# Routed attention and a cosine router on one core: gates of early blocks written ahead of a weight load, the first wide item's sums and rows ahead of the gates' parts

## The chip, the cores and the metric

One core of a Trainium2 chip runs the whole program in one launch. The core has five engines, each with its own list of instructions in a fixed order: PE (matmuls; PEld loads its stationary operand), DVE (element work and 32x32 transposes), ACT (activations and copies), POOL (element work, and DMAs whose rows are picked by a list of numbers) and SP (it only issues DMAs). An engine waits at an instruction until what it needs has come, and everything behind that instruction on the same engine waits too. The metric is the time of one execution in microseconds, as the median of several. Three runs before took 655.72 to 656.14, median 655.92.

## The reference

```python
# attention: every query sees only the keys of its own cluster
mask = q_assign[:, :, :, None] == k_assign[:, :, None, :]      # argmax over 16 unit centroids
scores = np.where(mask, scale * np.matmul(q, k.transpose(0, 1, 3, 2)), -1000000000.0)
attn = softmax(scores); x = np.matmul(attn, v)                 # (4, 8, 768, 64) -> rows (3072, 512)
# router: one of 8 experts for each row, by cosine
logits = xn @ en.T / tau
expert_idx = np.argmax(logits, axis=1); gate_w = probs[np.arange(N), expert_idx]
for e in range(E):                                             # w1[e]: 512x1024, w2[e]: 1024x512
    h = np.maximum(x[mask] @ w1[e], 0.0)
    out[mask] = gate_w[mask, None] * (h @ w2[e])
```

`softmax` stands for the three lines that shift, exponentiate and divide. All values are float32.

## The kernel before, in words

The attention works through 4 batches of 8 heads, 768 tokens each, and writes its rows to memory as `x_rows`. While it does, the rows of batches that are done are routed. Behind the attention come the experts, as a row of items, each with one expert's two weight tables, `w1s` and `w2s` (2 MB each, two buffers of each, loaded by `weights1` and `weights2`):

- Three early items (`E0[0]` to `E0[2]`) of 128 rows each, taken from the first 12 of 24 row blocks (`SA` of `NSLOT`), which are routed before the attention ends. Their work on PE is `hidden` (line 1653, 64 matmuls) and `result` (line 1694, 8 matmuls). The output rows are scaled by `gatein`, a gate for each row, and scattered to `out` by POOL.
- Eight sized (wide) items (`sized[0]` to `sized[7]`), one for each expert, of 392 down to 248 rows. Each product is done with seven half-size products in place of eight, so sums of quarters of the weights (`w1_sums`, lines 1390 to 1393) and of the rows (`x_sums`, lines 1365 to 1368) are made on DVE first.
- One block more at the end, and a branch (`overflow`) for rows that fit nowhere. With these inputs the branch isn't entered, but each engine loads `used` and compares.

The places of all rows are worked out by `Places(1)`, called `pb`, once the last batch is routed: `ranks`, `firsts` and `dest` on DVE; `hot_blocks` (`rr25b`, half on POOL at line 1026, half on DVE at line 1027) and `hot_rows` (`ohrb`, line 1033); `tokens`, 24 matmuls at line 1044 that turn these two into token numbers; `token_rows`, which writes the lists `gidx` and `sidx` by which POOL gathers the first wide item's rows (`collect`). The gates of all rows go the same way: `gate_parts` splits each gate into three bfloat16 parts, `hot_gates` (line 1071) makes the operand `rg25b`, and `gates` multiplies it (24 matmuls, line 1080). `spread_gates` (line 1622) lays the result out for the wide items.

The gates of the first three batches take a second way, for the early items: `gate_pieces` turns them, SP writes them to memory as `gate_rows` (line 809, four DMAs of 18 rows of 128 bytes), and `fetch_gate` gathers them on POOL (line 1138).

The first wide item's rows are not read back transposed. They are gathered on the chip, put in order by DVE (`order_rows`, line 1330) and turned by PE (`turn_rows`, line 1348). The rows of the second wide item are gathered, written to memory (`lay`, line 1243) and read back (`bring`, line 1260); SP can't issue the read before the write has landed.

What sets the order is the text of the kernel: `manual_schedule` is on for all five engines, so each engine's list is the order in which the calls stand. The engines meet only through semaphores.

Of the kernel before, what the change touches and what calls it, by code (L numbers as in the profile page):

```python
# [39 lines left out]
def kernel(  # L40
# [1136 lines left out]
    def weights1(it, parts=1):  # L1177
        it.e = expert_of(it)
        for i in range(parts):
            load_part(w1s[it.slot], moe_w1, it.e, KD, i, parts)  # L1180
# [98 lines left out]
    def fetch_gate(it):  # L1279
        gate = mo[it]["gate"] = xip.tile([P, 1], F32, tag="gatein", name="gatein", bufs=4)  # L1280
        gather(gate, gate_rows[0 : SA * P], gidxs[0][:, it.j : it.j + 1], SA * P)
# [7 lines left out]
    def turn_x(it, evict=None, xT=None):  # L1289
        d = mo[it]  # L1290
        if it.kind == "sized":
            n = WIDE[it.j]
            d["xT"] = szp.tile([P, KD, SQ * max(WIDE)], F32, tag="xTs", name="xTs", bufs=1)
            for u in range(0, n, NQ):
                m = min(NQ, n - u)
                nc.vector.transpose(
                    d["xT"][:, :, SQ * u : SQ * u + SQ * m].rearrange(
                        "p c (w t) -> p w c t", t=SQ
                    ),
                    d["xs"][:, u : u + m].rearrange("p w (c i) -> p w c i", i=SQ),  # L1300
                )
            return
        d["xT"] = mop.tile([P, DM], F32, tag="xTm", name="xTm") if xT is None else xT
        if it.kind == "block" or it in E0[1:]:
            nc.vector.transpose(
                d["xT"].rearrange("p (c w t) -> p w c t", c=KD, t=SQ),
                d["xin"].rearrange("p w (c i) -> p w c i", i=SQ),
            )
            return
        bk = psX.tile([P, DM], F32, tag="x_ps", name="x_ps")  # L1310
        for c in range(KD):
            nc.tensor.transpose(
                bk[:, P * c : P * c + P], d["rows"][:, c].rearrange("p w i -> p (w i)"), ident
            )
        evict(d["xT"], bk)

    def order_rows(it):

        d = mo[it]
        spare = szp.tile([P, max(WIDE), P], F32, tag="ys", name="ordered", bufs=YB)  # L1320
        spare = spare.rearrange("p u x -> p (u x)")
        d["ordered"] = []
        for i, (x, _) in enumerate(d.pop("rows_in")):
            n = x.shape[0]
            if DM * i + DM <= spare.shape[1]:
                to = spare[0:n, DM * i : DM * i + DM]
            else:
                to = szp.tile([P, FH, HC], F32, tag="hS1", name="ordered", bufs=1)
                to = to.rearrange("p f t -> p (f t)")[0:n, 0:DM]
            nc.vector.tensor_copy(  # L1330
                to.rearrange("p (c w i) -> p c w i", c=KD, w=NQ),
                x.rearrange("p (w c i) -> p c w i", c=KD, w=NQ),
            )
            d["ordered"].append(to)
# [35 lines left out]
    def x_sums(it):  # L1370

        d, h = mo[it], CAPS[it.j] // 2
        sums = d["xS"] = [
            szp.tile([P, KH, HC], F32, tag=f"xS{i}", name=f"xS{i}", bufs=1)[:, :, 0:h]
            for i in (1, 2, 4)
        ]
        four_sums(halves(it), sums)
# [6 lines left out]
    def w1_sums(it):  # L1384

        (b11, b12), (b21, b22) = quarters(w1s[it.slot])
        t2, t3, t4 = mo[it]["t1"] = [
            szp.tile([P, KH, F // 2], F32, tag=f"t1{i}", name=f"t1{i}", bufs=1) for i in (2, 3, 4)
        ]
        nc.vector.tensor_tensor(t3, b22, b12, ALU.subtract)  # L1390
        nc.vector.tensor_tensor(b12, b12, b11, ALU.subtract)
        nc.vector.tensor_tensor(t2, b22, b12, ALU.subtract)
        nc.vector.tensor_tensor(t4, b21, t2, ALU.subtract)
# [243 lines left out]
    def hidden(it, halves=(0, 1), span=(0, 512)):  # L1637

        d = mo[it]
        for half in halves:  # L1640
            if half == 0 and span[0] == 0:
                if it.kind == "whole":
                    t = szp.tile([P, KD, SQ * max(WIDE)], F32, tag="yT", name="hT", bufs=1)
                    d["hT"] = t.rearrange("p g t -> p (g t)")[:, 0:F]
                else:
                    d["hT"] = mop.tile([P, F], F32, tag="hT", name="hT")
            f0 = 512 * half
            if span[0] == 0:
                d["h_ps"] = psH.tile([P, 512], F32, tag="h_ps", name="h_ps")
            bk = d["h_ps"]  # L1650
            for m in range(*span, P):
                for c in range(KD):
                    nc.tensor.matmul(  # L1653
                        bk[:, m : m + P],
                        lhsT=w1s[it.slot][:, c, f0 + m : f0 + m + P],
                        rhs=d["xT"][:, P * c : P * c + P],
                        start=(c == 0),
                        stop=(c == KD - 1),
                    )
            if span[1] == 512:  # L1660
                nc.scalar.activation(d["hT"][:, f0 : f0 + 512], bk, ACTF.Relu)
# [99 lines left out]
    E0 = items[0:KA]  # L1761
    later = items[KA:]
    sized, last = later[:-1], later[-1]
# [70 lines left out]
    with tc.manual_schedule(engines=by_hand):  # L1834
        begin()
        for i in range(0, len(units), 2):
            n, it = divmod(i // 2, NJ)
# [51 lines left out]
        pb = Places(1, rtb)  # L1889
# [12 lines left out]
        hidden(E0[0], (1,), (0, 256))  # L1902
        products(0, 1)
        hidden(E0[0], (1,), (256, 512))
        weights1(E0[2])
        logits(0, 1)
        choose()
        for gate in gates[1:]:
            gate()
        for it in E0:  # L1910
            fetch_gate(it)
        hidden(E0[1], (0,), (0, 256))
        pb.ranks()
        hidden(E0[1], (0,), (256, 512))
        pb.firsts()
        pb.dest(0)
        pb.dest(1)
        pb.hot_blocks()
        turn_x(E0[2])
        hidden(E0[1], (1,))  # L1920
        for j in range(NJ):
            norms(j)
# [15 lines left out]
        pb.token_rows(gidxs[1], sidxs[1])  # L1938
        collect(sized[0])
        pb.experts(True)  # L1940
        for gate in gates[1:]:
            gate()
        pb.gate_parts()
        result(E0[1])
        w1_sums(sized[0])
        pb.hot_gates(NB)
        order_rows(sized[0])
        pb.gates(slot_gates)

        def overflow():  # L1950
            n_used = nc.values_load(used[0:1, 0:1], min_val=0, max_val=KX + NO)
# [34 lines left out]
        collect(sized[1])  # L1986
        result(E0[2], (2,), 4)
        turn_rows(sized[0])
        result(E0[2], (3,), 4)
        weights2(sized[0])  # L1990
        weights1(sized[1])
        lay(sized[1])
        bring(sized[1])
        spread_gates()
        x_sums(sized[0])

        next_of = dict(zip(sized, [*sized[2:], last]))
        for k, it in enumerate(sized[:-1]):
            after = sized[k + 1]
            before = sized[k - 1] if k else None  # L2000

            def first_steps(i):
                if i == 0:
                    if before:
                        sized_rows(before)
                        put(before)
                    if k:
                        collect(next_of[it])
                        w2_copy(it, "b11")
                elif i == 1 and k:  # L2010
                    w2_sum(it, "t3")
                elif i == 2 and k:
                    w2_copy(it, "b22")

            def second_steps(i):
                if i == 0:
                    h_sums(it, 0)
                    if k:
                        w2_sum(it, "t2")
                        w2_copy(it, "b21")  # L2020
                elif i == 1 and k:
                    w2_sum(it, "t4")
                elif i == 2 and k:
                    weights2(after)
                    send(before)
                elif i < 5 and not k:
                    w2_sum(it, ("t1", "t3", "t2", "t4")[i - 1])
                    if i < 4:
                        w2_copy(it, ("b11", "b22", "b21")[i - 1])
                    else:  # L2030
                        collect(next_of[it])
                        weights2(after)

            def third_steps(i):
                if i == 0:
                    h_sums(it, 2)
                    if after is not sized[-1]:
                        w1_sums(after)
                elif i == 1:
                    turn_x(after)  # L2040
                    bring(next_of[it])
                    weights1(next_of[it])
                elif i == 3 and after is not sized[-1]:
                    x_sums(after)
                elif i == 4 and after is not sized[-1]:
                    w2_sum(after, "t1")

            sized_hidden(it, 0, first_steps)
            sized_hidden(it, 2, second_steps)
            lay(next_of[it])  # L2050
            sized_result(it, third_steps)
# [68 lines left out]
```

## Time and profile before

| | us |
|---|---|
| median of 3 runs (655.72 to 656.14) | 655.92 |
| the profiled execution | 657.54 |
| its span | 655.8 |
| PE busy | 636.8 (97%) |
| DVE busy | 497.4 (76%) |
| ACT busy | 316.9 (48%) |
| POOL busy | 164.5 (25%) |

The granted TensorE clock is 0.988 of full speed over the span. The page cuts the span into 40 slices of 16.4 us and gives each engine's busy share in tenths; a timeline gives, for each run of like instructions, its start, its length, the engine, the line, what it writes and reads, and in brackets how long the engine sat idle before it and what ended that. All times within the span are counted from its start. Lengths of matmuls reach from the first start to the modelled end of the last; a group followed without a gap ends a little after the next has begun.

### The profile page before, as it was taken

To read this page: it belongs to the slowest core of one execution; us is meant where nothing else is said; L and a number is where in the kernel's file an instruction comes from. 1 tells how busy PE (TensorE), PEld (TensorE's weight loads), DVE (VectorE), ACT (ScalarE), POOL (GpSimd) and SP (SyncE) were. 2 spreads that over 40 slices of the span, in tenths; PEclk is the share of its full clock that TensorE was granted. 3 is DMA by queue.
4 is the path that set the end of the run, shared out by engine and by line. 5 is a ranking of instruction groups with operands and counts; after the bars stand their busy time and mean duration, and the time that the engine had idled before them with its cause. 6 is when DMAs were issued, how large, how long until landed. Compare 5 with 4: busy or idle time off the path is not lost. (4 is left out here: it accounts for less than half of the span.)

```text
span 655.8 us, 16397 instructions
## 1 busy us (share of the span) xinstructions
PE 636.8 (97%) x6529; PEld 451.8 (69%) x6529; DVE 497.4 (76%) x823; ACT 316.9 (48%) x533; POOL 164.5 (25%) x360
## 2 busy tenths in 40 slices
PE   9999999999999999999995799999999999999997
PEld 4444444444444445445675369999999999999995
DVE  6988988998889999999884628677777778775210
ACT  6656655677655785667541125152525242433311
POOL 2222212312214112235704412205040404030111
PEclk9999999999999999999997899999999999999999
DMA  9855666787549678667888258877996969685753
GB/s 153 127 89 102 99 94 106 154 144 122 102 82 171 132 160 171 132 158 210 259 224 298 85 158 288 267 252 229 310 294 224 302 220 300 234 289 209 253 164 111
DMA packets 257665, 122.62 MB, mean 187 GB/s; under 512 B 208257, under 2 KB 228609, under 8 KB 257580
## 3 DMA queue, kind: packets, MB, share of 16 engines
q1 hardware_dynamic: 253116, 108.58, 65.9%
q0 software_dynamic: 4288, 12.85, 6.2%
q8 instruction: 54, 0.88, 0.6%
q14 instruction: 31, 0.25, 0.1%
q10 hardware_dynamic: 176, 0.05, 0.0%
HBM read 92.53 MB, written 23.28 MB: 177 GB/s over the span
## 5 line engine op out<-in xcount | busy, mean ns | idle before, releaser
L585 ACT ACTIVATE prob<-s_ps 128x768 f32<-128x768 f32 x192 | 154.3, 813 | 100.1 <-PE s_ps L574 97.5
L574 PE MATMUL s_ps<-qT,kT 64*64 64x384 f32 x1536 | 156.1, 483 | 0.0
L596 PE MATMUL o_ps<-prob,v 64*64 64x385 f32 x1536 | 141.3, 484 | 0.0
L615 DVE TENSOR_TENSOR acc<-acc,prob 128x768 f32<-128x768 f32 x128 | 121.4, 948 | 8.6
L596 PEld LDWEIGHTS o_ps<-prob,v 64*64 64x64 f32 x1536 | 57.6, 133 | 65.5 <-issue 58.0
L574 PEld LDWEIGHTS s_ps<-qT,kT 64*64 64x64 f32 x1536 | 55.2, 133 | 36.1 <-issue 31.9
L1149 POOL DMA_INDIRECT out_dram<-rows_out,sidx x24 | 25.4, 1059 | 169.0 <-DMA rows_out<-y_slots 165.4
L574 PE MATMUL s_ps<-hot 64*64 64x384 bf16 x768 | 64.4, 325 | 0.0
L574 PEld LDWEIGHTS <-hot 64*64 64x64 bf16 x768 | 23.9, 106 | 42.4 <-issue 40.6
L630 POOL COPY behind<-acc 1x1 f32<-1x1 f32 x30 | 6.6, 222 | 158.7 <-DVE acc L615 154.3
L664 POOL COPY inv<-inv 32x12 f32<-32x12 f32 x120 | 31.5, 262 | 38.3 <-DVE inv L660 34.0
L1608 DVE STREAM_TRANSPOSE ys<-yT 128x352 f32<-128x352 f32 (+4 forms) x32 | 14.2, 498 | 33.8 <-ACT yT L1596 21.9
L1138 POOL DMA_INDIRECT rows_in<-x_rows,gidx x25 | 27.4, 1098 | 35.2 <-DMA x_slots<-rows_in 26.6
L1653 PE MATMUL h_ps<-xTm,w1s 128*128 128x128 f32 x256 | 31.8, 285 | 1.5 <-DMA w1s<-in_moe_w_dram 1.5
L605 DVE SCALAR_TENSOR_TENSOR acc<-prob,prob 128x768 f32<-128x768 f32 x32 | 33.2, 1037 | 0.0
L1653 PEld LDWEIGHTS h_ps<-xTm,w1s 128*128 128x128 f32 x256 | 30.6, 199 | 3.5 <-issue 3.5
L620 ACT COPY o_sb<-o_ps 128x770 f32<-128x770 f32 x32 | 25.6, 800 | 9.5 <-PE o_ps L596 9.5
L1454 ACT COPY u<-h_ps 128x344 f32<-128x344 f32 (+5 forms) x22 | 9.6, 438 | 40.3 <-PE h_ps L1547 25.3
L632 POOL TENSOR_TENSOR o_sum<-o_sb 128x385 f32<-128x385 f32 x30 | 25.7, 857 | 1.5 <-ACT o_sb L620 0.9
L1694 PE MATMUL y_ps<-w2s,hT 128*128 128x512 f32 x48 | 23.1, 629 | 0.2 <-PEq L1966 0.2
L1454 ACT COPY u<-y_ps 128x344 f32<-128x344 f32 (+5 forms) x20 | 8.8, 438 | 29.5 <-PE y_ps L1547 17.7
L1459 ACT ACTIVATE h<-h 128x344 f32<-128x344 f32 (+5 forms) x42 | 20.1, 484 | 5.3 <-DVE h L1476 2.7
(357 smaller groups left out, 1157.8 us busy)
## 6 DMA issues: line engine op xcount, KB each, us to landing
w1s<-in_moe_w_dram SPq DMA_DIRECT2D x10, 2048.0 KB
w2s<-in_moe_w_dram SPq DMA_DIRECT2D x10, 2048.0 KB
q<-in_q_dram SPq DMA_DIRECT2D x64, 96.0 KB
k<-in_k_dram SPq DMA_DIRECT2D x64, 96.0 KB
x_rows<-xb SPq DMA_DIRECT2D x64, 96.0 KB
v<-in_v_dram SPq DMA_DIRECT2D x120, 48.0 KB
xr<-x_rows SPq DMA_DIRECT2D x9, 512.0 KB
rows_out<-y_slots SPq DMA_DIRECT2D x17, 256.0 KB
```

What stands on the lines that cost most here:

```text
L574: nc.tensor.matmul(s_ps[D * half : D * half + D, h, 0:HS], lhsT=l[rows, half], rhs=r[rows], start=part == (1 if len(parts) < 2 else 0), st ...
L585: nc.scalar.activation(d["prob"][:, :, 0:HS], d["s_ps"][:, :, 0:HS], ACTF.Exp, scale=scale)
L596: nc.tensor.matmul(g["o_ps"][D * h : D * h + D, half, 0:HE], lhsT=ld[n]["v"][keys, j, h], rhs=d["prob"][keys, h, 0:HE], start=(j == 0), st ...
L605: nc.vector.scalar_tensor_tensor(out=g["acc"], in0=un[i - 1]["prob"][:, :, 0:HS], scalar=NJ * EPS, in1=d["prob"][:, :, 0:HS], op0=ALU.add, ...
L615: nc.vector.tensor_tensor(g["acc"], g["acc"], d["prob"][:, :, 0:HS], ALU.add)
L620: nc.scalar.copy(t["o_sb"], g["o_ps"][:, :, 0:HE])
L632: add(t["o_sum"][:, hq], t["o_sb"][:, 0], t["o_sb"][:, 1], ALU.add)
L664: copy(inv2[M * to : M * to + M, :, i % 2], inv[M * i : M * i + M])
L1138: nc.gpsimd.indirect_dma_start(out=to, out_offset=None, in_=of, in_offset=bass.IndirectOffsetOnAxis(ap=at, axis=0), bounds_check=n - 1, oo ...
L1149: inst = nc.gpsimd.indirect_dma_start(out=to, out_offset=bass.IndirectOffsetOnAxis(ap=at, axis=0), in_=of, in_offset=None, bounds_check=n - 1,
L1653: nc.tensor.matmul(bk[:, m : m + P], lhsT=w1s[it.slot][:, c, f0 + m : f0 + m + P], rhs=d["xT"][:, P * c : P * c + P], start=(c == 0), stop ...
L1694: nc.tensor.matmul(bk, lhsT=d["hT"][:, P * c : P * c + P], rhs=w2s[it.slot2][:, c], start=(c == 0), stop=(c == KF - 1),)
```

## The change

Only the order of calls changes; nothing is computed that was not computed before. `weights1(E0[2])` stands behind the gates' pieces, which issue `gate_rows`. Only the first early item's gate is gathered ahead of `hot_blocks`, the other two behind it. `turn_x(E0[2])` stands ahead of `firsts`. `w1_sums` and `order_rows` of the first wide item stand ahead of the last piece of the last batch's gates (`gates[3]`), and the gates' parts and products behind. The gates' matmuls go behind `turn_rows` and `x_sums`, `spread_gates` goes between two products of the first wide item, and `weights1(sized[1])` behind `lay` and `bring`. `own_gates` keeps the operand, since `overflow` makes one of its own.

```diff
         hidden(E0[0], (1,), (256, 512))
-        weights1(E0[2])
         logits(0, 1)
         choose()
         for gate in gates[1:]:
             gate()
-        for it in E0:
-            fetch_gate(it)
+        weights1(E0[2])
+        fetch_gate(E0[0])
         hidden(E0[1], (0,), (0, 256))
         pb.ranks()
         hidden(E0[1], (0,), (256, 512))
+        turn_x(E0[2])
         pb.firsts()
         pb.dest(0)
         pb.dest(1)
         pb.hot_blocks()
-        turn_x(E0[2])
+        for it in E0[1:]:
+            fetch_gate(it)
         hidden(E0[1], (1,))
...
         pb.experts(True)
-        for gate in gates[1:]:
-            gate()
-        pb.gate_parts()
+        gates[1]()
+        gates[2]()
         result(E0[1])
         w1_sums(sized[0])
+        order_rows(sized[0])
+        gates[3]()
+        pb.gate_parts()
         pb.hot_gates(NB)
-        order_rows(sized[0])
-        pb.gates(slot_gates)
+        own_gates = pb.rg
...
         turn_rows(sized[0])
+        x_sums(sized[0])
+        pb.rg = own_gates
+        pb.gates(slot_gates)
         result(E0[2], (3,), 4)
         weights2(sized[0])
-        weights1(sized[1])
         lay(sized[1])
         bring(sized[1])
-        spread_gates()
-        x_sums(sized[0])
+        weights1(sized[1])
...
-                elif i == 1 and k:
+                elif i == 1 and not k:
+                    spread_gates()
+                elif i == 1:
                     w2_sum(it, "t3")
```

SP around the third early item's weights (`w1s_58`), before, and then after the change. `xr` are the last batch's rows for the norms, `e_early` the expert's number.

```order
L748 DMA xr<-x_rows 128x6x32 x4
L1173 TENSOR_LOAD e_early
L1173 ISA x2
L1188 ISA
L1188 DMA w1s_58<-in_moe_w_dram 128x4x1024
L809 DMA gate_rows<-gate_t 18x32 x4
```

```order
L748 DMA xr<-x_rows 128x6x32 x4
L809 DMA gate_rows<-gate_t 18x32 x4
L1173 TENSOR_LOAD e_early
L1173 ISA x2
L1188 ISA
L1188 DMA w1s_58<-in_moe_w_dram 128x4x1024
```

The four writes of the gates have moved ahead of the expert's number and the 2 MB load.

DVE between the scale of the last batch's gates and the gates' operand, before, and then after. `t_...` are the sums of `w1s_59`, the first wide item's weights.

```order
L793 TENSOR_TENSOR lg_all<-lg_all,sq_all 128x48
L800 TENSOR_REDUCE gate_p<-lg_all 128x6
L801 TENSOR_SCALAR gate_p<-gate_p 128x6
L802 RECIPROCAL gate_p<-gate_p 128x6
L1061 CAST gsb<-gate_p 128x24
...
L1390 TENSOR_TENSOR t_5258<-w1s_59 128x1024
L1391 TENSOR_TENSOR w1s_59<-w1s_59 128x2x512
L1392 TENSOR_TENSOR t_5257<-w1s_59 128x1024
L1393 TENSOR_TENSOR t_5259<-w1s_59,t_5257 128x1024
L1071 TENSOR_TENSOR rg25b<-bm25b,gsb 128x24x25 x3
L1330 COPY ordered<-rows_in 128x512 x3
```

```order
L793 TENSOR_TENSOR lg_all<-lg_all,sq_all 128x48
L1390 TENSOR_TENSOR t_5248<-w1s_59 128x1024
L1391 TENSOR_TENSOR w1s_59<-w1s_59 128x2x512
L1392 TENSOR_TENSOR t_5247<-w1s_59 128x1024
L1393 TENSOR_TENSOR t_5249<-w1s_59,t_5247 128x1024
L1330 COPY ordered<-rows_in 128x512 x3
L1330 COPY ordered<-rows_in 32x512
L800 TENSOR_REDUCE gate_p<-lg_all 128x6
L801 TENSOR_SCALAR gate_p<-gate_p 128x6
...
L1065 CAST gsb<-grestb 128x24
L1071 TENSOR_TENSOR rg25b<-bm25b,gsb 128x24x25 x3
```

The four weight sums and the four copies of rows have moved ahead of the gates' sum, their five parts and the three products.

SP behind the branch: the second wide item's weights (`w1s_58`) and its rows, before, and then after.

```order
L1188 DMA w2s_60<-in_moe_w_dram 128x8x512
L1173 TENSOR_LOAD e_sized
L1173 ISA x2
L1188 ISA
L1188 DMA w1s_58<-in_moe_w_dram 128x4x1024
L1243 DMA x_slots<-rows_in 128x512 x2
L1243 DMA x_slots<-rows_in 96x512
L1260 DMA xs<-x_slots 32x11x128 x4
```

```order
L1188 DMA w2s_60<-in_moe_w_dram 128x8x512
L1243 DMA x_slots<-rows_in 128x512 x2
L1243 DMA x_slots<-rows_in 96x512
L1260 DMA xs<-x_slots 32x11x128 x4
L1173 TENSOR_LOAD e_sized
L1173 ISA x2
L1188 ISA
L1188 DMA w1s_58<-in_moe_w_dram 128x4x1024
```

The load has moved behind the write of the rows and behind their reading back.

## The prediction

> **What bounds the kernel now.** I read the page's slices first, then PE's waits, then PE's timeline where the slices dip.
>
> ```profile
> span 655.8 us, 16397 instructions
> PE   9999999999999999999995799999999999999997
> PE h_ps L1511 <- DVE xS L1365: 0.2, 1, 0.2
> ```
>
> A slice is 16.4 us: PE is full everywhere but in slices 22 and 23 (344 to 377 us), the passage from attention to the sized experts. The third row is PE's whole list of waits from 387 us to the end: 0.2 us. So behind 387.44 every microsecond is PE work, and what the passage saves should reach the end.
>
> ```profile
> 337.66 7.03 PE L1694 MATMUL y_ps<-w2s,hT 128*128 128x512 f32 x16
> 346.18 2.02 PE L1653 MATMUL h_ps<-xTm,w1s 128*128 128x128 f32 x16 [1.49 <-DMA w1s<-in_moe_w_dram]
> 353.68 0.66 PE L1044 MATMUL misc<-rr25b,ohrb 128*128 128x50 bf16 x12 [5.49 <-POOL rr25b L1026]
> 354.17 3.38 PE L1653 MATMUL h_ps<-xTm,w1s 128*128 128x128 f32 x16
> 357.39 0.47 PE L1044 MATMUL misc<-rr25b,ohrb 128*128 128x50 bf16 x12
> 357.70 3.82 PE L1653 MATMUL h_ps<-xTm,w1s 128*128 128x128 f32 x32
> 361.35 7.03 PE L1694 MATMUL y_ps<-w2s,hT 128*128 128x512 f32 x16
> 373.21 1.68 PE L1080 MATMUL misc<-rg25b,ohrb 128*128 128x75 bf16 x24 [4.83 <-DVE rg25b L1071]
> 374.69 5.06 PE L1694 MATMUL y_ps<-w2s,hT 128*128 128x512 f32 x8
> 379.91 1.95 PE L1694 MATMUL y_ps<-w2s,hT 128*128 128x512 f32 x4 [0.15 <-PEq L1966]
> 381.70 0.60 PE L1348 MATMUL x_ps<-ident,ordered 128*128 128x128 f32 x4
> 383.46 1.98 PE L1694 MATMUL y_ps<-w2s,hT 128*128 128x512 f32 x4
> 385.38 0.32 PE L1622 MATMUL misc<-g3b,identb 128*32 128x72 bf16 x16
> 385.63 1.59 PE L1511 MATMUL h_ps<-xTs,w1s 128*128 128x196 f32 x8
> 387.44 1.56 PE L1511 MATMUL h_ps<-xS,w1s 128*128 128x196 f32 x8 [0.22 <-DVE xS L1365]
> ```
>
> In brackets stands PE's idle time and what ended it. Two waits are large: 5.49 us for the POOL half of the token numbers' operand, 4.83 us for the gates' operand. Behind each the same work also runs slower: 16 matmuls of L1653 take 3.38 us at 354.17 and 2.02 at 346.18; 8 of L1694 take 5.06 us against half of 7.03.
>
> ```profile
> 343.40:346.80 3.40, 1.92 (x9) 0.88 (x8) 3.37 (x4) 2.17 (x4) 0.00 (x0) 1.00 0.76 271
> 346.80:350.20 3.40, 1.40 (x13) 1.23 (x12) 2.83 (x5) 0.00 (x0) 2.39 (x3) 1.00 1.01 359
> 350.20:353.60 3.40, 0.00 (x0) 0.00 (x0) 0.00 (x0) 0.29 (x1) 3.06 (x4) 0.50 1.04 362
> ```
>
> These are busy times by stretch; third from the right is the granted clock. It falls to 0.50 at 350.2, two microseconds after PE stopped.
>
> **The change, part by part.** First the gates' rows, now ahead of the weights `w1s` of the third early item.
>
> ```profile
> 338.38 0.39 SPq L1188 DMA_DIRECT2D w1s<-in_moe_w_dram  x1
> 338.81 1.51 SPq L809 DMA_DIRECT2D gate_rows<-gate_t  x4
> 347.64 2.08 POOL L1138 DMA_INDIRECT gatein<-gate_rows,gidx  x1 [22.23 <-DMA gate_rows<-gate_t]
> 352.43 1.20 POOL L1026 TENSOR_TENSOR rr25b<-bm25b,tok_lo 128x600 bf16<-128x600 bf16 x1
> 345.47 3.38 DVE L1033 TENSOR_TENSOR ohrb<-io_b,lob 128x1536 bf16<-128x1536 bf16 x2
> L776 POOL TENSOR_TENSOR cumx<-cumx,eq x18: 198/201/997, 123.3 to 282.6; 128x8 bf16<-128x8 bf16 x18
> ```
>
> Today four small writes stand behind 2 MB of weights, POOL waits 22.23 us for them, and the product `rr25b` stands behind three gathers. After: the writes go out at about 337.6, one gather follows, and `rr25b` starts when DVE is ready, about 345. The transpose of the third item moves from between the hot tables to ahead of `firsts`, so the order's end on DVE doesn't move. The two gathers behind `rr25b` feed scales that are wanted only when the second and third results end.
>
> `rr25b` now runs beside DVE's hot tables. An 8-column add on POOL took 198 ns at the least and 997 at the most, so company can cost 0.8 us; at worst `rr25b` waits for both hot tables and is ready at 348.9 + 1.2 = 350.1. PE asks for it at 349.5 (its first result ends at 337.66 + 7.03 = 344.69, then the new gap of 3.00 and 16 matmuls, 1.83): 0 to 0.6, taken as 0. The wait of 5.49 goes.
>
> What it costs: `w1s` is issued 1.51 us later. PE waited for these weights already, so the gap before the third item's first matmuls grows from 1.49 to 3.00. Below: 1.5, if the queue was held by the transfers ahead; above: 4.5, if small writes hold the engines again as long.
>
> A gap of 3.00 is a new clock risk. The clock stayed at 1.00 past a stretch with 1.92 us of work in 3.4 and fell past one with 1.40; the new gap, unless a stretch's boundary cuts it in halves, leaves less than 1.40 in one. Price: 3.38 less 2.02 is 1.36, 5.06 less 3.44 is 1.62; I take 1.5, bounds 0 and 2.
>
> The Trainium skill ("TensorE: Matmul & The Clock Gate", Part 1: The HAM clock gate) says that the clock halves after an idle window of about 3.4 us; by that rule a gap of 3.00 costs nothing and the sum would lose its 1.50 for the clock. The rows say otherwise here: the gap was 2.0 us old when the clock halved, so the measurement decides.
>
> Second, the first wide item's sums and rows (`w1_sums`, `order_rows`) ahead of the gates' last step, and PE's 24 gate matmuls behind `turn_rows`.
>
> ```profile
> 357.89 0.21 DVE L1054 COPY tk25b<-misc 128x50 f32<-128x50 f32 x1 [8.20 <-PE misc L1044]
> 360.55 0.21 DVE L793 TENSOR_TENSOR lg_all<-lg_all,sq_all 128x48 f32<-128x48 f32 x1
> 364.28 0.20 DVE L800 TENSOR_REDUCE gate_p<-lg_all 128x6 f32<-128x48 f32 x1 [3.52 <-issue]
> 366.08 1.23 DVE L1390 TENSOR_TENSOR t<-w1s 128x1024 f32<-128x1024 f32 x1
> 371.00 2.16 DVE L1071 TENSOR_TENSOR rg25b<-bm25b,gsb 128x600 bf16<-128x600 bf16 x3
> 373.08 1.41 DVE L1330 COPY ordered<-rows_in 128x512 f32<-128x512 f32 x4
> 358.00:359.00 1.00, 1.00 (x11) 1.00 (x10) 0.86 (x7) 0.18 (x1) 0.00 (x0) 1.00 0.36 143
> 359.00:360.00 1.00, 1.00 (x11) 1.00 (x10) 0.90 (x6) 0.00 (x0) 0.76 (x1) 1.00 0.00 0
> ```
>
> DVE's list behind the scale: sums 4.92 (366.08 to 371.00), rows 1.41, gate sum and parts 1.80 (364.28 to 366.08), products 2.16: 10.29 us in any order. It can't start before the first wide item's `w1s` lands. Transfers fall silent at 359 (last row), so it lands by then; after, 1.5 us later, and the four row gathers (0.8 MB, 2.2 us at the 362 GB/s above) share the engines: 360.1 to 362.3, taken as 360.8. The token copy moves to 353.5 and the scale, 2.9 later, to 356.4, so both are earlier than that. The gates' operand is ready at 371.1.
>
> Now PE from 344.69 to its second wide product, today 387.44: 42.75 us. Work at full clock, start to start: 64 `hidden` matmuls 7.30 (32 from 357.70 to 361.35), 24 for tokens 0.62 (12 in 0.31), 32 for results 13.76 (0.43 each), rows turned 1.76 (381.70 to 383.46), 24 for gates 0.74 (half of 1.48, 373.21 to 374.69, run at half clock), the first wide product 1.40, the spreading of the gates 0.25, which now stands behind the second product. Sum 25.83. With the gap 3.00, the clock 1.50 and the branch 0.15: 30.48. Gain 42.75 - 30.48 = 12.27.
>
> PE reaches the gates at 344.69 + 3.00 + 1.50 + 0.15 + 7.92 + 12.04 + 1.76 = 371.06, level with the operand at 371.1. So either may end last; 0.5 is taken for that, with 0 and 1.5 as bounds. If the clock stays full, PE comes at 369.6 and waits till 371.1: the same end. Gain 11.8.
>
> Third, SP's order: `w1s` of the second wide item goes behind its rows' way through memory.
>
> ```profile
> 385.48 0.39 SPq L1188 DMA_DIRECT2D w2s<-in_moe_w_dram  x1
> 387.25 1.93 SPq L1243 DMA_DIRECT2D x_slots<-rows_in  x3
> 402.82 1.85 SPq L1260 DMA_DIRECT2D xs<-x_slots  x4
> 408.02 1.22 DVE L1390 TENSOR_TENSOR t<-w1s 128x1024 f32<-128x1024 f32 x1
> 415.94 0.57 DVE L1471 TENSOR_TENSOR yT<-h_ps,u 128x392 f32<-128x392 f32 x1 [1.18 <-PE h_ps L1547]
> ```
>
> `w2s` goes out at about 373.7. Today the rows are back for reading 17.34 us later, behind 4 MB of weights; with 2 MB fewer (5.8 us at 362 GB/s) 11.5 us, at 385.2. SP stands still until then, reads for 1.85, loads the expert's number and issues `w1s` at 387.9; with 7.8 us as at 338.38 to 346.18, and 1.9 for the reads ahead, it lands at 395.7 to 397.6. DVE wants it at 408.02 - 11.8 = 396.2. So it is at most 1.4 late; DVE has 1.18 idle before its next sum for PE. Cost 0, bounds 0 and 2. What queues behind it on SP, the next `w2s`, is wanted later still.
>
> The profiled execution took 657.54 with a span of 655.8; the median shown is 655.92. The gain is a difference within the span and comes off the median: 644.1.
>
> **Rivals.** *Weights late*: the first wide `w1s` lands at 364, because gathers and weights share engines; the operand comes at 374.3, 3.2 late: 647.3. For: the transfers run at share 1.04 there. Against: the gathers are small. *The rows come no sooner*: the writes land at 347.64 as now, since the loads ahead of them are slow; with one gather ahead `rr25b` is ready at 350.9 instead of 349.5, 1.4 of the wait stays: 645.5. Against: today 2 MB stand ahead of them. *Full clock and early weights*: a stretch's boundary cuts the gap in halves, the first wide `w1s` lands at 359.5, the operand is there at 369.8 and PE at 369.6: 642.3. For: the stretch with 1.92 kept the clock. Against: few boundaries fall so. The rule quoted from the Trainium skill would lead to the same end. *Slower than before*: SP held by the rows. If the second wide `w1s` lands after about 397.4 + 1, DVE's sums, and with them the second wide item on PE, slip one for one; the loss passes the gain at 398.4 + 11.8 = 410.2, 22 us after its issue. For: today's rows took 17.34. Against: the 4 MB that they waited for are gone.
>
> **How the numbers follow.** Forecast 644.1, own range 642.8 to 645.4: 0.58. Weights late 0.17, rows no sooner 0.07, full clock 0.09, slower 0.04, the rest, a mishap that I don't see, 0.05. Range 642.3 to 647.6. A measurement here tells 0.2% (1.3 us) from no change: faster 0.93, same 0.03, slower 0.04.
>
> **What would show it.** Right: POOL's wait before the first `gatein` falls from 22 to about 16 us and `rr25b` runs near 345; PE waits about 3 us for `w1s` and hardly for `rr25b`; the gates' matmuls follow the turned rows without more than 1 us of wait; the second wide product starts near 375; behind it PE's waits stay under 1 us. Wrong: a wait of PE for `rr25b`, `rg25b` or `ordered` over 2 us, or a wait in the second wide item that leads back to `w1s`.

## The result and the profile after

The changed kernel took 645.4 us (644.58 to 647.64, 6 runs) beside 656.03 for the kernel before (654.75 to 656.40, 6 runs): ratio 0.9845, 95% interval 0.9827 to 0.9863. The forecast was 644.1 with a range of 642.3 to 647.6. The profiled execution took 645.84 with a span of 644.1; the spans differ by 11.7, and the forecast of this difference was 11.8.

The page of the changed kernel, its span and PE's slices, and below it PE's waits from 337 us to the end (in total, times, longest):

```profile
span 644.1 us, 16396 instructions
PE   8999999999999999999999899999999999999997
```

```profile
PE misc L1080 <- DVEq L1968: 2.8, 1, 2.8
PE misc L1044 <- POOL rest L1134: 1.1, 1, 1.1
PE y_ps L1694 <- PEq L1968: 0.2, 1, 0.2
```

Both large waits have shrunk, from 5.5 to 1.1 for the token numbers and from 4.8 to 2.8 for the gates, and the one for `w1s` is gone. PE's timeline shows what became of the passage (start, length, what runs, idle time before it):

```profile
337.11 7.03 PE L1694 MATMUL y_ps<-w2s,hT 128*128 128x512 f32 x16
343.98 1.95 PE L1653 MATMUL h_ps<-xTm,w1s 128*128 128x128 f32 x16
347.08 0.48 PE L1044 MATMUL misc<-rr25b,ohrb 128*128 128x50 bf16 x12 [1.15 <-POOL rest L1134]
...
366.23 1.40 PE L1348 MATMUL h_ps<-ident,ordered 128*128 128x128 f32 x12
370.41 1.68 PE L1080 MATMUL misc<-rg25b,ohrb 128*128 128x75 bf16 x24 [2.79 <-DVEq L1968]
371.89 2.66 PE L1694 MATMUL y_ps<-w2s,hT 128*128 128x512 f32 x4
374.39 1.49 PE L1511 MATMUL h_ps<-xTs,w1s 128*128 128x196 f32 x8
375.72 1.49 PE L1511 MATMUL h_ps<-xS,w1s 128*128 128x196 f32 x8
```

The last row is the second wide product, at 387.44 before: 11.72 earlier. From there to the end of the span it is 268.38 us, and it was 268.36, so all that the change does has been done by this row. The matmuls behind the gates run at half speed. The same shows in the windows of this execution, where the third column from the right is the granted clock:

```profile
366.50:369.90 3.40, 1.13 (x11) 0.94 (x10) 3.16 (x12) 1.10 (x2) 2.01 (x3) 1.00 0.09 18
369.90:373.30 3.40, 2.89 (x26) 2.29 (x26) 3.12 (x7) 0.00 (x0) 1.74 (x3) 0.50 0.58 186
```

On DVE stands the list that the gates wait for, in its new order: sums, rows, gate sum and parts, products.

```profile
360.27 1.23 DVE L1390 TENSOR_TENSOR t<-w1s 128x1024 f32<-128x1024 f32 x1 [7.73 <-SPq L1968]
365.20 1.42 DVE L1330 COPY ordered<-rows_in 128x512 f32<-128x512 f32 x4
366.54 0.18 DVE L800 TENSOR_REDUCE gate_p<-lg_all 128x6 f32<-128x48 f32 x1
368.14 2.16 DVE L1071 TENSOR_TENSOR rg25b<-bm25b,gsb 128x600 bf16<-128x600 bf16 x3
```

The list takes 10.0 us (360.27 to 370.30; 10.29 were forecast) and starts when the first wide item's `w1s` is there, as forecast. But DVE stands idle for 7.73 us ahead of it, and its last two rows need no weights at all. On POOL the first gather and the operand, and DVE's hot tables beside it:

```profile
336.48 0.99 POOL L1138 DMA_INDIRECT gatein<-gate_rows,gidx  x1 [11.01 <-DMA gate_rows<-gate_t]
343.69 1.72 POOL L1026 TENSOR_TENSOR rr25b<-bm25b,tok_lo 128x600 bf16<-128x600 bf16 x1 [6.21 <-DVE bm25b L1023]
345.36 1.71 POOL L1134 COPY rest<-rest 1x1 f32<-1x1 f32 x1
344.27 4.42 DVE L1033 TENSOR_TENSOR ohrb<-io_b,lob 128x1536 bf16<-128x1536 bf16 x2
```

The wait for `gate_rows` fell from 22.23 to 11.01, and `rr25b` no longer stands behind three gathers. The tables, 3.38 us before, take 4.42 with POOL's product beside them.

### The profile page after: what moved, and what is told of

The parts are those of the page before. It is cut to its first block, busy times and chain, and to the rows that moved or that the text cites. A ratio compares the mean times of both kernels' runs of the same rounds, so it can differ in the third digit from the quotient of the medians.

```text
span 644.1 us, 16396 instructions
## 1 busy us (share of the span) xinstructions
PE 633.5 (98%) x6529; PEld 450.0 (70%) x6529; DVE 498.3 (77%) x823; ACT 316.9 (49%) x533; POOL 168.5 (26%) x360
## 5 line engine op out<-in xcount | busy, mean ns | idle before, releaser
L1138 POOL DMA_INDIRECT rows_in<-x_rows,gidx x25 | 30.1, 1203 | 31.3 <-DMA x_slots<-rows_in 26.1
L1653 PE MATMUL h_ps<-xTm,w1s 128*128 128x128 f32 x256 | 30.4, 277 | 0.0
```

The source lines that it names most:

```text
L1138: nc.gpsimd.indirect_dma_start(out=to, out_offset=None, in_=of, in_offset=bass.IndirectOffsetOnAxis(ap=at, axis=0), bounds_check=n - 1, oo ...
L1653: nc.tensor.matmul(bk[:, m : m + P], lhsT=w1s[it.slot][:, c, f0 + m : f0 + m + P], rhs=d["xT"][:, P * c : P * c + P], start=(c == 0), stop ...
```

## The experiments

Twelve runs were made, in four groups: ten further kernels, and two of the kernels a second time. Each group has its own runs of the kernel before (medians 655.75, 656.36, 656.45, 656.64). Within each kernel the executions differ by 0.6 to 5 us, so a difference of 1 us between two groups decides nothing by itself; where it matters the profile is read.

### The gates' rows alone

```diff
 # on the kernel before: the first part of the change, nothing else
-        weights1(E0[2])
         logits(0, 1)
...
-        for it in E0:
-            fetch_gate(it)
+        weights1(E0[2])
+        fetch_gate(E0[0])
...
+        turn_x(E0[2])
         pb.firsts()
...
-        turn_x(E0[2])
+        for it in E0[1:]:
+            fetch_gate(it)
```

> Only the first part of the change on the kernel before: rows of gates written ahead of the weights, one gather ahead of rr25b, the transpose moved. The two parts share one goal, so they are not additive. Theory: the token wait of 5.49 us shrinks to about 1.2 and its slow clock (1.4) goes, but PE then comes to the gates' product at about 360 and waits there longer than before, until the first wide w1s has landed (360.3 in the profile after) and sums (4.9) and products (2.2) are done, about 367.4. The gates' product starts at 367 instead of 373: about 6 us faster than before, 650. Rival (each part worth its own wait): 5.5 + 1.4 = 7 us faster, 649, with the wait for rg25b still 4.8.

Measured: 653.42 (651.81 to 653.71), ratio 0.9958 [0.9943, 0.9973]. Two rows of PE's timeline, and the windows behind the stall:

```profile
347.15 0.48 PE L1044 MATMUL misc<-rr25b,ohrb 128*128 128x50 bf16 x12 [0.67 <-POOL rest L1134]
...
369.23 1.68 PE L1080 MATMUL misc<-rg25b,ohrb 128*128 128x75 bf16 x24 [8.88 <-DVE rg25b L1071]
```

```profile
363.70:367.10 3.40, 0.00 (x0) 0.00 (x0) 3.33 (x4) 0.00 (x0) 1.82 (x2) 0.51 0.00 1
367.10:370.50 3.40, 1.27 (x21) 1.27 (x21) 3.40 (x7) 0.00 (x0) 2.93 (x4) 0.50 0.42 100
370.50:373.90 3.40, 3.40 (x11) 1.70 (x9) 0.82 (x5) 0.00 (x0) 0.26 (x1) 0.50 0.38 117
```

The token wait falls from 5.49 to 0.67, but 4.05 of the 4.82 us saved come back at the gates, whose wait grows from 4.83 to 8.88, and the clock is halved for 10 us there. Only 2.3 us are left. The theory had the mechanism and not the time (650): the gates' matmuls start at 369.23 where it had 367, since the first wide weights are there at 362.09 and not at 360.3. The rival (649, with the gates' wait as before) fails on both. Earlier token numbers are worth little while the gates' operand waits for the first wide `w1s`.

### Everything but the gates' rows

The changed kernel with the first part undone (the diff above, backwards).

> The changed kernel with the first part undone (weights first, three gathers ahead of rr25b). Theory: the token wait of 5.5 us is back, but behind it nothing of the gates is late: DVE has its sums, rows and products done by about 371.5 while PE works on results until 373.5, so no wait for rg25b or ordered over 1 us. The second wide product starts at about 379 (375.7 in the profile after, 387.4 before): 8 us faster than before, 648, so 3 slower than the change. Rival (the parts are additive): the change without 5.5 + 1.4, so 652.

Measured: 648.39 (647.79 to 648.98), 0.9883 [0.9867, 0.9899]. From PE's timeline and DVE's:

```profile
351.68 0.66 PE L1044 MATMUL misc<-rr25b,ohrb 128*128 128x50 bf16 x12 [4.66 <-POOL rr25b L1026]
...
374.77 1.05 PE L1080 MATMUL misc<-rg25b,ohrb 128*128 128x75 bf16 x24
```

```profile
344.82 3.38 DVE L1033 TENSOR_TENSOR ohrb<-io_b,lob 128x1536 bf16<-128x1536 bf16 x2
```

The token wait is back and hides the gates' wait altogether. The second and third part alone are worth 7.4, the first alone 2.3, and both together 10.6. The hot tables take 3.38 on DVE as in the kernel before; they come back to this below.

### The second wide item's weights back ahead of its rows

```diff
+        weights1(sized[1])
         lay(sized[1])
         bring(sized[1])
-        weights1(sized[1])
```

> The changed kernel with the second wide item's w1s issued again ahead of its rows. Theory: in the profile after, DVE waits 3.8 us for these weights and PE doesn't, so the move costs nothing and gives nothing: within 1 us of the change, 645.4, with DVE's wait for w1s gone and a later read of the rows. Rival (the late weights cost PE time by way of DVE): 1 to 3 us faster than the change.

Measured: 648.3 (645.23 to 650.00), 0.9877 [0.9854, 0.9901]. On DVE the second wide sums start without a wait; on PE the second wide product:

```profile
399.58 1.22 DVE L1390 TENSOR_TENSOR t<-w1s 128x1024 f32<-128x1024 f32 x1
```

```profile
378.62 1.49 PE L1511 MATMUL h_ps<-xS,w1s 128*128 128x196 f32 x8
```

In the changed kernel DVE waits 3.76 us for these weights, until 400.52. The wait is gone here, and yet PE needs 268.4 us from 378.62 to the end of the span (647.0), the same as with it. So in this profile the third part costs and brings nothing behind this row. The median is 2.9 higher, outside both expectations. In the profile the loss lies ahead of this row (PE waited 1.39 for the third early item's `w1s`, the first wide weights came 1.1 later, and the clock was halved twice as long), where this edit moves nothing; the changed kernel once more, further below, is nearly as late (647.36). That the other executions are late for the same reason is likely and not shown.

### The gates first on DVE, then on PE too

```diff
+        gates[3]()
+        pb.gate_parts()
+        pb.hot_gates(NB)
+        own_gates = pb.rg
         w1_sums(sized[0])
         order_rows(sized[0])
-        gates[3]()
-        pb.gate_parts()
-        pb.hot_gates(NB)
-        own_gates = pb.rg
```

In a second kernel PE's 24 gate matmuls also stand ahead of `turn_rows`. That one ran first:

> The changed kernel with the gates' last step, parts and products ahead of the first wide item's sums on DVE (DVE stands idle 7.7 us there for w1s), and the gates' product ahead of the turned rows on PE. Theory: rg25b is ready at about 359.5, so PE's 2.8 us wait and its slow clock (1.6) go; the turned rows wait for ordered for under 1 us. The second wide product starts at about 371.4 instead of 375.7: about 4 us faster than the change, 641. Rival (what is short there is DVE's total, 10.3 us behind the weights in any order): no gain, 645, with a wait of 2 to 3 us for ordered in place of rg25b.

Measured: 643.32 (642.74 to 647.06), 0.9820 [0.9797, 0.9843]. This is 2.1 under the 645.4 of the changed kernel, between the theory (641) and the rival (645). In the profiled execution, one of the slower ones of this kernel (span 645.2), the gates don't wait, and PE is late by itself:

```profile
347.82 3.75 PE L1653 MATMUL h_ps<-xTm,w1s 128*128 128x128 f32 x16 [3.73 <-DMA w1s<-in_moe_w_dram]
...
371.08 1.04 PE L1080 MATMUL misc<-rg25b,ohrb 128*128 128x75 bf16 x24
```

This is the gap for the third early item's `w1s` that was forecast as 3.00, with the halved clock behind it (3.75 for 16 matmuls). It is 3.73 here and 0 in the changed kernel's profile, though both kernels are the same up to this place. To see how much such executions differ, the changed kernel ran once more beside three others:

> The changed kernel once more, beside the three others on one chip. Theory (the wait for the third early item's w1s differs from execution to execution, 0 in the first profile, up to 3.7 in a neighbour's): a median of 645.4 with single runs from 644 to 648, and a profile in which the matmuls of L1653 wait 0 to 3 us for w1s, while the wait for rg25b is there in each execution, 1 to 3 us. Rival (the 10 us list on DVE sets the end alone): the same end whatever the first wait was, runs within 0.5 us of each other.

Measured: 647.36 (646.26 to 648.03), 0.9856 [0.9834, 0.9877]. DVE's first wide sums, and PE's two stops behind them:

```profile
361.71 1.23 DVE L1390 TENSOR_TENSOR t<-w1s 128x1024 f32<-128x1024 f32 x1 [9.18 <-SPq L1968]
```

```profile
367.19 0.63 PE L1348 MATMUL x_ps<-ident,ordered 128*128 128x128 f32 x4 [1.41 <-DVE ordered L1330]
...
372.12 1.04 PE L1080 MATMUL misc<-rg25b,ohrb 128*128 128x75 bf16 x24 [3.06 <-DVEq L1968]
```

The weights land 1.44 later than in the first profile, and the gates follow 1.71 later, though they were asked for at the same time (350.7). In this execution the transfer's records show 15 of its 16 parts done by 360.35 and the last at 361.69. So this profile is late for another reason than the expectation named: its wait for the third early item's `w1s` is only 0.39. The ten runs of both sets have a median of 646.4. Now DVE's order alone:

> The gate sum, the parts and the three products of rg25b go ahead of the first wide item's sums and rows on DVE; PE's order stays as changed. Theory (these 4 us need no weights and fit the 7.7 us in which DVE stands idle ahead of 360.3): the operand is ready near 364, PE's wait of 2.8 us for it goes, and with it the halved clock at 370 to 373: 642.5, at most 644. Rival (the rows, now behind the gates, become what PE waits for, since the sums still begin at 360.3 at the earliest): the wait comes back on ordered, 1 to 2 us, and the time stays near 645.

Measured: 643.44 (642.21 to 646.77), 0.9810 [0.9784, 0.9836], 3.9 under the changed kernel on the same chip. DVE, then PE:

```profile
358.90 2.16 DVE L1071 TENSOR_TENSOR rg25b<-bm25b,gsb 128x600 bf16<-128x600 bf16 x3
362.63 1.23 DVE L1390 TENSOR_TENSOR t<-w1s 128x1024 f32<-128x1024 f32 x1 [1.57 <-SPq L1968]
```

```profile
346.87 2.02 PE L1653 MATMUL h_ps<-xTm,w1s 128*128 128x128 f32 x16 [2.20 <-DMA w1s<-in_moe_w_dram]
...
368.12 0.63 PE L1348 MATMUL x_ps<-ident,ordered 128*128 128x128 f32 x4 [0.68 <-DVE ordered L1330]
...
369.91 1.05 PE L1080 MATMUL misc<-rg25b,ohrb 128*128 128x75 bf16 x24
```

The products are done at 361.06, in the time in which DVE stood idle. The gates' wait is gone, the rows' is 0.68, and this with weights that landed 2.4 later than in the changed kernel's first profile. What left the list behind `w1s` is the 1.60 of gate sum and parts (366.54 to 368.14) and the 2.16 of products, 3.8 in all. That the gain of 3.9 is just as large is in part chance: the halved clock is gone as well, the weights landed at different times, and against all ten runs of the changed kernel (646.4) the gain is 2.9. But the wait for the gates is gone, as the theory said.

### The weights of the third early item first

The second of these kernels (gates first on DVE and PE), with the 2 MB issued ahead of `gate_rows` again, and all three gathers behind `rr25b`:

```diff
         hidden(E0[0], (1,), (256, 512))
+        weights1(E0[2])
         logits(0, 1)
...
-        weights1(E0[2])
-        fetch_gate(E0[0])
...
         pb.hot_blocks()
-        for it in E0[1:]:
+        for it in E0:
             fetch_gate(it)
```

> The gates' products ahead of the sums on DVE and ahead of the turned rows on PE, as in the run of 643.3, and the third early item's w1s issued ahead of the gates' rows again, as in the kernel before, with all three gathers behind rr25b. Theory (what is left is the wait for w1s, 0 to 3.7 us with a halved clock behind the long ones, and it is long because w1s stands behind the rows): the wait is 0 to 1.5, the clock stays full ahead of 350, all runs lie near 641.5 to 642.5. Rival (the traffic ahead of w1s on SP's queue differs by itself, the rows are a small part): the spread stays and the median is 643.

Measured: 642.66 (642.30 to 645.16), 0.9799 [0.9778, 0.9820]; it ran beside the 647.36. Once more, in the next group:

> The kernel that took 642.66 once more, beside the two others. Theory: 642.3 to 643.2, with at most a quarter of its runs over 644. Rival (the first set was lucky, and the wait for w1s spreads as in the changed kernel): a median of 643.5 to 645.

Measured: 643.21 (642.90 to 643.49, 6 runs), 0.9795 [0.9766, 0.9825], with hardly any spread in this group. Its two medians are the lowest of the study, and it is called the fastest kernel below; but the two kernels with the gates first (643.32 and 643.44) lie within 1 us of it, so what this edit adds to them isn't shown. From its second profile:

```profile
344.08 1.95 PE L1653 MATMUL h_ps<-xTm,w1s 128*128 128x128 f32 x16
347.48 0.48 PE L1044 MATMUL misc<-rr25b,ohrb 128*128 128x50 bf16 x12 [1.46 <-DVE ohrb L1033]
...
367.02 1.04 PE L1080 MATMUL misc<-rg25b,ohrb 128*128 128x75 bf16 x24 [0.81 <-DVEq L1967]
```

The wait for `w1s` was 0.71 in the first profile and is 0 here. The same edit to the changed kernel, with the gates left where the change put them:

> The changed kernel with the third early item's w1s issued ahead of the gates' rows and all three gathers behind rr25b; the gates' work stays behind the sums and rows. Theory (DVE's list behind the first wide w1s sets PE's next stop, so PE, arriving sooner, only waits longer for rg25b): the wait for w1s is at most 1.5, the wait for rg25b 2.5 to 4, the median 645 to 646, as with the changed kernel. Rival (the wait for w1s is what lies between this kernel and the one with 642.7): 643 to 643.5.

Measured: 646.23 (644.17 to 647.19), 0.9832 [0.9801, 0.9864], 3.0 over the kernel with gates and weights first, beside which it ran.

```profile
344.64 1.95 PE L1653 MATMUL h_ps<-xTm,w1s 128*128 128x128 f32 x16
...
371.44 1.68 PE L1080 MATMUL misc<-rg25b,ohrb 128*128 128x75 bf16 x24 [2.81 <-DVEq L1967]
```

PE comes without a gap and waits 2.81 at the gates, as the theory said: while the gates stand at the end of DVE's list, earlier weights for the third item bring nothing that can be told.

### The operand's POOL half on DVE

```diff
-            nc.gpsimd.tensor_tensor(self.rr[:, :, 1], bm, bc(tok_lo[:, 0:n], shp, 2), ALU.mult)
+            own = nc.gpsimd if self.part == 0 else nc.vector
+            own.tensor_tensor(self.rr[:, :, 1], bm, bc(tok_lo[:, 0:n], shp, 2), ALU.mult)
```

On the changed kernel:

> POOL's half of the token numbers' operand rr25b is written by DVE instead (0.7 us there, a third of the 2.16 for three such products). Theory (POOL's product and DVE's hot tables hinder each other: the two tables took 4.42 us beside it and 3.38 alone): the tables take 3.4 again, the wait of 1.15 us at the token matmuls falls to 0.8 or less, and the time by 0.3 to 0.5: 645.0. Rival (POOL itself is late, as the profile's releaser says): the wait goes altogether and the time is 644.2.

Measured: 649.34 (647.24 to 650.35), 0.9890 [0.9872, 0.9909], 2.0 slower than the changed kernel beside it. On the kernel with gates and weights first:

> The kernel that took 642.66 (gates first on DVE and PE, w1s ahead of the gates' rows), with POOL's half of rr25b on DVE as well. Theory (the hot tables run 1.0 us faster alone and DVE has 0.7 more to do): the tables take 3.4, the token matmuls wait 0.3 less, 642.3 to 642.7. Rival (putting that product on DVE costs by itself, as the 649.3 of its first trial says): 644.5 or more.

Measured: 644.42 (643.32 to 645.95), 0.9812 [0.9781, 0.9844], 1.2 slower than the same kernel without it. DVE and PE of this last one:

```profile
345.44 3.41 DVE L1034 TENSOR_TENSOR ohrb<-io_b,lob 128x1536 bf16<-128x1536 bf16 x2
362.37 1.22 DVE L1391 TENSOR_TENSOR t<-w1s 128x1024 f32<-128x1024 f32 x1 [1.80 <-SPq L1968]
```

```profile
347.24 0.48 PE L1045 MATMUL misc<-rr25b,ohrb 128*128 128x50 bf16 x12 [1.21 <-DVE ohrb L1034]
```

The local half of the theory holds: the tables take 3.41 where they took 4.42 beside POOL's product, and the token matmuls wait 1.21 in place of 1.46, 0.25 less. Yet both kernels are slower. In the profile the first wide `w1s` is there at 362.37, 1.8 later than in the kernel beside it, and this one profile can't tell whether the edit does that (POOL, freed, issues its row gathers 3 us sooner, at 352.20 against 355.31) or chance. The landing records don't settle it: 15 of the load's 16 parts are in by 360.60 here and by 358.38 in the first profile of the fastest kernel, where the gathers start at 355.32; but in the kernel with everything but the gates' rows the load is in only at 361.09, though the gathers start at 357.81. The first kernel's profile, of the fastest of its six executions, shows a wait of 3.67 for the third early item's `w1s`; its slower executions weren't profiled. Why the edit costs 1 to 2 us stays open.

### The gate matmuls ahead of the branch

On the fastest kernel, `pb.gates(slot_gates)` moves up, to stand directly ahead of `overflow()`.

> The kernel that took 642.66 and 643.21, with PE's 24 gate matmuls ahead of the branch for overflowing experts instead of behind it. Theory (PE's wait of 0.5 to 0.8 at those matmuls, which the trace puts to DVE's queue at the branch, is for DVE to come past the branch with all of its list, and not for rg25b, which is ready near 360.2): no wait for rg25b, since PE comes there after 364; the turned rows follow once ordered is there, and the second wide product starts near 371.5 instead of 372.4 to 372.8: 642.0 to 642.5. Rival (the matmuls wait for rg25b itself): a wait there as before, 642.7 to 643.2.

Measured: 646.99 (645.05 to 649.02), 0.9857 [0.9834, 0.9880]: both expectations missed. The profiled execution is the slowest of the five, and PE also waits 2.04 in it for the third early item's `w1s`, with a halved clock behind; so how much of the loss in the median is the branch isn't shown. In the first profile of the fastest kernel, and then in this one:

```profile
366.60 1.04 PE L1080 MATMUL misc<-rg25b,ohrb 128*128 128x75 bf16 x24 [0.46 <-DVEq L1967]
```

```profile
366.05 1.04 PE L1080 MATMUL misc<-rg25b,ohrb 128*128 128x75 bf16 x24
370.73 3.41 PE L1694 MATMUL y_ps<-w2s,hT 128*128 128x512 f32 x4 [3.64 <-PEq L1967]
```

The gates don't wait, so what they waited for behind the branch wasn't `rg25b` (ready at 360.2 in the first profile of the fastest kernel, where they still waited until 366.60) but DVE's whole list. That part of the theory holds. But the branch itself now costs PE 3.64 us, and the halved clock follows. With eight result matmuls (3.44 us) directly ahead of it the branch showed as 0.15. The branch has rows of its own in the trace (durations in ns, then when the first and the last began). In the first profile of the fastest kernel, PE's branch and DVE's signal behind it:

```profile
L1967 PEldq COMPARE_BRANCH  x1: 4612/4612/4612, 357.1 to 357.1; - x1
L1967 DVEq EVENT_SEMAPHORE  x1: 21/21/21, 366.5 to 366.5; - x1
```

And PE's branch in this kernel:

```profile
L1967 PEldq COMPARE_BRANCH  x1: 3612/3612/3612, 366.9 to 366.9; - x1
```

DVE's signal comes at 366.5 and PE's gates start at 366.60, so it is DVE's list that they waited for. And the branch isn't cheaper in one place than in another: it takes PE's sequencer 3.3 to 6.3 us in all fourteen profiles, against 0.05 to 0.07 on each other engine. Elsewhere the sequencer is at the branch while long matmuls that it has already issued still run: at 357.1 in the fastest kernel, where PE works on until 366.14. Behind the 24 short ones it gets there at 366.9, when PE has 0.2 us of work left. Why the branch takes PE so long is open. The Trainium skill ("Runtime: NRT & Kernel Launch", Instruction fetch mechanics) says that a taken branch out of the fetched pages forces a fetch before execution goes on. The 3.6 us would agree with that, but no row here ties a fetch to PE.

## Why the prediction was right, point by point

**What bounds the kernel.** Right: the stretch behind the second wide product is 268.3 to 268.6 us long in eleven of the thirteen profiles of changed kernels (268.36 before). It is 267.9 with the gates' rows alone, where `spread_gates` still stands ahead of the product, and 269.3 with the operand on DVE and everything else moved, with 0.7 of a wait for ACT behind the product.

**Gates' rows early, token wait gone.** Right in mechanism. The wait didn't fall to the 0 that was taken but to 1.15, past the upper bound of 0.6. Neither POOL nor the rows were late for that: the term for POOL and DVE hindering each other was put on POOL's side alone, and the runs showed it on both, with the price on DVE's. POOL's product takes 1.72 in place of 1.20 beside the hot tables, and they take 4.41 to 4.42 in every profile with it and 3.38 to 3.42 without. The first of the two tables takes 2.75 in place of 1.75 and ends at 347.02, and PE starts at 347.08. The profile's releaser, a copy of one number on POOL that took 1.71 in place of 0.18, is a witness of the same and not the cause: in the fastest kernel the same wait stands against `ohrb`. The Trainium skill ("SBUF — State Buffer", SBUF: two separate sides) says that DVE operations with two inputs from that memory and POOL lock a shared port for whole instructions; the 1.0 us that DVE loses to a product of 1.2 to 1.7 us is of that size.

**The gap of 3.00 and the clock, 1.50.** Mis-sized: both were 0 in the first profile. In the seven profiles in which the gates' rows stand ahead of this load the gap is between 0 and 3.73, 1.7 in the mean; in the changed kernel's two it is 0 and 0.39. What varies is when SP gets to this load: at 335.82 in the first profile, at 339.99 in the one with 3.73. The 1.51 of four writes was added to the old time of SP's list, 338.38, as if this time were fixed; with the old order back (everything but the gates' rows) it was 334.70.

**The list on DVE, "10.29 us in any order".** The size was right (10.03), the start too (360.27 against 360.8), and so was the operand's time (370.30 against 371.1). What failed is "in any order" behind the weights: gate sum, parts and products need no `w1s`. The kernel with them ahead of the sums gained 3.9 beside the changed one, 2.9 against all its ten runs. It was overlooked that the diff itself moves this work behind the weights, from a list in which only the products stood there.

**PE level with the operand, 0.5 for that.** PE came 3.4 us earlier than forecast (367.62 against 371.06: no gap and no halved clock, 4.50 less, and 1.15 more for the tokens) and waited 2.79. The alternative that the working names, that PE waits and the end is the same, is what happened, but the price of such a wait was left out: it halves the clock for the gates and four results. They take 1.48 and 2.50 from start to start, against 0.74 in the forecast and 1.79 in the kernel with DVE's gates first: 1.45. The operand 0.8 earlier than forecast, the 0.5 that wasn't needed and the clock 1.45 dearer nearly cancel. So the second wide product at 375.72, where 375.64 was forecast, is in part luck: three terms (the gap, its clock and the 0.5) came to nothing, and two that the sum doesn't have (1.15 for the tokens, the clock behind the gates' wait) came in their place, with a wait of 2.79.

**SP's order, cost 0.** Right, with a larger delay than its bounds: DVE waits 3.76 for the second wide `w1s`, not 1.4 at most, and PE still loses nothing.

**Base and median.** The difference of the spans came out as 11.7 (11.8 forecast), that of the medians as 10.6. The profiled execution before took 657.54, 1.5 over the median of its group of runs; the profiled one after is 0.4 over its own. That is 1.1 of the 1.3 by which 645.4 misses 644.1. The forecast is closer than the kernel is steady: the second set's median is 647.36, that of all ten runs 646.4, 2.3 over the forecast.

**Criteria.** By the prediction's own list one sign of being wrong appeared, a wait for `rg25b` over 2 us, and it was right to put it there: it points to the 2 to 4 us that the change left on the table (643.4 against 645.4, 646.4 or 647.36). Of the signs of being right, PE's wait of about 3 us for `w1s` and gates that follow without a wait didn't come; the second wide product near 375 and the short waits behind it did. Some executions of the changed kernel go part of the way to the rival *Weights late*: in the second set, with the weights there at 361.71, PE waits 1.41 for the rows and 3.06 for the gates.

## What to carry to other kernels

When a list of work on one engine waits for a late transfer, sort it by what needs that transfer: whatever doesn't goes into the idle time ahead, and only the rest counts from the landing. Removing one of two stalls in a row moves most of it to the next (here 4.05 of 4.82 us), so price the pair. A wait of PE behind a branch can be for everything that another engine has ahead of the same branch, and it has a second price in the clock. A branch that isn't entered can still cost an engine microseconds (3.3 to 6.3 on PE here), so put long work that is already issued ahead of it.

## What was not expected of the hardware

The clock's price isn't tied to the length of the gap alone. PE's idle times of 2.04 us (gate matmuls ahead of the branch), 2.79 and 3.73 were followed by a clock of 0.50 to 0.57 in the windows, while 2.20 (DVE's gates first) and 3.01 (operand on DVE, 365.96 to 368.97) left it at 1.00; all these windows are 3.4 or 4 us wide. In the changed kernel's second profile the clock fell only at about 373.3, 1.2 us after PE had started again. What the falls have in common is a stretch with little work: between 340 and 380 us the fourteen profiles have twelve falls, and in each the 3.41 us ahead of the fall hold at most 1.42 us of PE's work, and the clock stays low for one, two or three times 3.41 us. Where such stretches begin may decide which gap is dear; no run here sets that. The Trainium skill ("TensorE: Matmul & The Clock Gate", Part 1: The HAM clock gate) puts the halving behind an idle window of about 3.4 us; idle times of 2.04 and 2.79 halved it here, so that is not enough of a rule for this kernel.

A load of 2 MB is as late as the last of its 16 parts: in the second set of the changed kernel that came 1.34 us behind the other fifteen (0.18 in its first profile), and DVE's list, which sets the passage's end, starts with it.
